# Second DFT step along S as products of 64x64 quadrants instead of 128x128 tables

## The chip, the cores and the metric

The kernel runs on one core of a Trainium2 chip. The metric is the time of one execution on the device in microseconds (us); the median of several runs is compared. The engines are named as in the profile: PE is TensorE (matmul), PEld its weight load, DVE is VectorE, ACT is ScalarE, POOL is GpSimd, and SP is SyncE, whose queue issues nearly all DMA transfers here.

## The reference, cut to what matters

One training step of a small network block, forward and backward, in bfloat16, with S = 2048 rows and D = 448 columns:

```
h   = x + irfft2(rfft2(layernorm(x)) * (w_r + 1j * w_i))        # part A, a spectral filter
h2  = h + B(layernorm(h))                                       # part B: MLP along S, 2048 -> 1792 -> 2048, gelu
outputs: h2, and the gradients of x, w_r, w_i, w1, b1, w2, b2 for a given grad_out
```

The transforms are two-dimensional: along D (448 points, real input, so 225 frequencies) and along S (2048 points). Part A needs one forward and one inverse transform in the forward pass, and one forward and one inverse transform again in the backward pass, where also the gradient of the filter is formed.

## The kernel before

**The DFT as matmuls.** The transform along S is split as 2048 = 128 x 16. A first step (`row_a`, `row_b`) does the part along D and one factor of the part along S, and its results go by DMA into the tile `D2`: 128 partitions, 16 groups, and per group a real and an imaginary row of 226 frequencies. The second step along S handles each of the 16 groups `g` by a table of its own: the real table `Vt[:, g, :]`, the imaginary table `Ut[:, g, :]` and the latter's negative `Un[g]`, each 128x128. A product with a complex operand is three matmuls that add into one PSUM buffer: 452 columns by V (real and imaginary part at once), then 226 columns by U and 226 columns by -U:

```
mm(pv, lhsT=Vt[:, g, :], rhs=D2[:, g, :, :], start=True, stop=False)
mm(pv[:, 0, :], lhsT=Ut[:, g, :], rhs=D2[:, g, 1, :], start=False, stop=False)
mm(pv[:, 1, :], lhsT=Un[g], rhs=D2[:, g, 0, :], start=False, stop=True)
```

In the order of rows and columns used here, the entries of a table that aren't zero are spread over the whole of it; most entries are zero. `gen_UV` builds Ut and Vt while the first step runs (16 masked copies of 128x256 elements at line 508 or 510, shared between DVE and ACT); `gen_inv_s` makes the inverse tables UTt, VTt from them by products with the permutation `permI`; `gen_neg` makes the negatives on DVE.

**The stage.** `s2_stage` runs this step twice, once in the forward pass (`make_inv` true) and once in the backward pass. It loops over `c2`, a pair of groups. In one turn it does the forward product of two groups, copies the result out of PSUM (`evac`) into `xs[c2]`, does the inverse product (`s2_inv`) of two groups that were multiplied by the filter some turns before, copies that out and sends it to `D3` by DMA. After this, `on_mult` multiplies a pair by the filter: `w_mult` is four `tensor_tensor` operations on DVE per pair, two of 904 and two of 452 elements per partition; in the backward pass there are four more for the filter's gradient. The multiplication of a pair follows `ml` turns after its forward product (`ML_F` = 4 in the forward pass, 0 in the backward pass), the inverse product two turns after that.

**What fills PE.** `fill(n)` takes the next n matmuls of a pending generator, here `dg_gen` (a product of part B's backward pass with w2, 224 matmuls of 448 columns) in the forward pass, and `gw_gen` (weight gradients, mostly 512 columns) in the backward pass. Each turn of the stage fills 2 x 3 matmuls in the forward pass, 2 x 8 in the backward pass. What is left of `dg_gen` runs after the stage (`drain`). Every engine's order is the order of the program's text, except POOL's, which a scheduler decides.

**Who copies.** `evac` puts each copy on ACT or DVE, whichever has the smaller estimated load so far; this is decided when the program is built. POOL isn't used by `evac`.

**The filter.** `w_load` brings w_r and w_i by eight DMA transfers into `W_rows`: four while the first step runs, and four at the start of the stage. `w_place` copies it into the order of the frequencies (`W_view_F`): 16 copies of 64 partitions x 900 elements, by `evac`, four per turn in turns 3 to 6. In the backward pass the filter comes back from memory (`w_d`), and the gradient is stored by eight transfers (`w_io`) from inside the last stage (`gx_consumer`, turns `GW_AT`).

Of the kernel before, what the change touches and what calls it, by code (L numbers as in the profile page):

```python
# [17 lines left out]
P = 128  # L18
# [6 lines left out]
NT = 16  # L25
# [97 lines left out]
def kernel(  # L123
# [98 lines left out]
    def v4(ap):  # L222
        return ap.rearrange("p (b c) -> p b c", b=4)
# [18 lines left out]
    Ut = mem.tile([P, NG, P], BF16, name="Ut")  # L242
    Vt = mem.tile([P, NG, P], BF16, name="Vt")
    UTt = mem.tile([P, NG, P], BF16, name="UTt")
    VTt = mem.tile([P, NG, P], BF16, name="VTt")
# [3 lines left out]
    permI = mem.tile([P, P], BF16, name="permI")  # L249
# [101 lines left out]
    for _ in range(26):  # L351
# [5 lines left out]
    gp_.iota(fr.rearrange("p (c q i g) -> p c q i g", c=2, q=2, i=4), pattern=[[1, 2], [8, 2], [16, 4], [2, 4]], base=0,  # L357
             channel_multiplier=0, allow_small_or_imprecise_dtypes=True)
# [72 lines left out]
    def gen_R(ve, sc):  # L431
        t = ftmp(2688, P).bitcast(I32)
        tv = t.rearrange("p (c h x) -> p c h x", c=4, h=2)
        f2 = fr.rearrange("p (c x) -> p c x", c=4)
        for h in range(2):
            ve.tensor_scalar(out=tv[:, :, h, :], in0=f2, scalar1=pcol, scalar2=96.0 + 32.0 * h, op0=ALU.mult, op1=ALU.add)
        ve.tensor_scalar(out=tv[:, 0, 1, 0:1], in0=pcol, scalar1=64.0, scalar2=96.0, op0=ALU.mult, op1=ALU.add)
        ve.tensor_scalar(out=t, in0=t, scalar1=127, scalar2=None, op0=ALU.bitwise_and)
        sc.activation(out=Rm[:], in_=t, func=ACT.Sin, scale=s128, bias=half_r)


    def decode(eng):
        a4, fc, s_, c_, f_ = col(), col(), col(), col(), col()
        floor_div(eng, a4, pcolb, 32)
        gp_madd(s_, a4, -32.0, pcolb)
        floor_div(eng, fc, s_, 4)
        gp_madd(s_, fc, -4.0, s_)
        gp_madd(s_, s_, 4.0, a4)
        floor_div(eng, c_, fc, 4)
        gp_madd(f_, c_, -4.0, fc)  # L450
        return fc, s_, c_, f_

    def masks(eng, c_, f_):
        msk, mk, k0, k1 = col(4), col(), col(), col()
        for j in range(4):
            eng.tensor_scalar(out=msk[:, j:j + 1], in0=f_, scalar1=float(j), scalar2=None, op0=ALU.is_equal)
        eng.tensor_tensor(out=mk, in0=msk[:, 0:1], in1=c_, op=ALU.mult)
        eng.tensor_scalar(out=k1, in0=mk, scalar1=-1.0, scalar2=1.0, op0=ALU.mult, op1=ALU.add)
        eng.tensor_tensor(out=k0, in0=mk, in1=msk[:, 0:1], op=ALU.subtract)
        eng.tensor_scalar(out=k0, in0=k0, scalar1=1.0, scalar2=None, op0=ALU.add)  # L460
        return msk, mk, k0, k1
# [3 lines left out]
    def gen_UV():  # L465
        _, s_, c_, f_ = rows = decode(gp_)
        nrow = col()
        gp_madd(nrow, rows[0], 16.0, s_)
        msk, mk, k0, k1 = masks(gp_, c_, f_)
# [12 lines left out]
        ve.tensor_scalar(out=permI[:], in0=krow[:, 0:P], scalar1=nrow, scalar2=None, op0=ALU.is_equal)  # L482
        ve.scalar_tensor_tensor(out=base[:, 0, :, 1], in0=fix, scalar=mk, in1=base[:, 0, :, 1], op0=ALU.mult, op1=ALU.add)
        for dst, o0, o1, pt in ((Ut, ou, ou, pu), (Vt, ov0, ov1, pv)):
            t = ftmp(1024 if dst is Ut else 2048, 16, 16, 2).bitcast(I32)
            for k, o in ((0, o0), (1, o1)):
                ve.tensor_scalar(out=t[:, :, :, k], in0=base[:, :, :, k], scalar1=s_, scalar2=o,
                                 op0=ALU.mult, op1=ALU.add)
                yield
            ve.tensor_scalar(out=t[:, 0, :, 1], in0=base[:, 0, :, 1], scalar1=s_, scalar2=pt, op0=ALU.mult, op1=ALU.add)  # L490
# [4 lines left out]
            sc.activation(out=comp, in_=t.rearrange("p g l c -> p (g l c)"), func=ACT.Sin, scale=s2048, bias=half_uv)  # L495
            yield True
            cv = comp.rearrange("p (g l c) -> p g l c", g=16, l=16)
            for c, k in ((1, k0), (0, k1)):
                ve.tensor_scalar(out=cv[:, 0, :, c], in0=cv[:, 0, :, c], scalar1=k, scalar2=None, op0=ALU.mult)
            yield  # L500
            d0 = dst[:, :, 0:64].rearrange("p g (l f) -> p g l f", f=4)
            d1 = dst[:, :, 64:112].rearrange("p g (l f) -> p g l f", f=3)
            for j in range(4):
                m = msk[:, j:j + 1]
                dj = d1[:, :, :, j - 1] if j else dst[:, :, 112:128]
                for o, c in ((d0[:, :, :, j], 0), (dj, 1)):
                    if load[1] + 0.24 < load[0] + 0.38:
                        ve.tensor_scalar(out=o, in0=cv[:, :, :, c], scalar1=m, scalar2=None, op0=ALU.mult)
                    else:
                        sc.activation(out=o, in_=cv[:, :, :, c], func=ACT.Copy, scale=m)  # L510
                    yield
# [7 lines left out]
    def gen_inv_s(h):  # L519
        src, dst = ((Ut, UTt), (Vt, VTt))[h // 4]  # L520
        g0 = 4 * (h % 4)
        pt = ps_ff()
        for i in range(4):
            mm(pt[:, i * P:(i + 1) * P], lhsT=src[:, g0 + i, :], rhs=permI[:], start=True, stop=True)
        evac(out=dst[:, g0:g0 + 4, :].rearrange("p g c -> p (g c)"), in_=pt[:])
# [37 lines left out]
    def w_io(Wv, dr, di, store):  # L563
        for c_, d in ((0, dr), (1, di)):
            for p0, p1, g0, g1, row, dims in ((0, 64, 0, 16, 0, [[16 * DF, 4], [1, 16 * DF]]),
                                              (64, 112, 0, 16, 112, [[-DF, 48], [1, DF]]),
                                              (112, 128, 1, 16, 127, [[-DF, 15], [1, DF]]),
                                              (112, 128, 0, 1, 64, [[1, DF]])):
                sb = Wv[p0:p1, g0:g1, c_, 0:DF]
                d_ap = bass.AP(d.tensor, d.offset + row * DF, [[P * DF, 16]] + dims)  # L570
                if store:
                    nc.sync.dma_start(out=d_ap, in_=sb)
                else:
                    nc.sync.dma_start(out=sb, in_=d_ap)
# [4 lines left out]
    def w_load():  # L579
        for c_, d in ((0, A_w_r), (1, A_w_i)):  # L580
            for p0, p1, j0, j1, row, dims in ((0, 64, 0, 16, 0, [[16 * DF, 4]]), (64, 112, 0, 16, 97, [[-16 * DF, 3]]),
                                              (112, 128, 0, 15, 113, []), (112, 128, 15, 16, 64, [])):
                nc.sync.dma_start(out=W_rows[p0:p1, c_, j0:j1, :],
# [4 lines left out]
    def w_place():  # L588
        for g in range(0, NG, 4):
            for c_ in range(2):  # L590
                for p0, p1, src in ((0, 64, W_rows[0:64, c_, g:g + 4, :]),
                                    (64, P, W_rows[64:P, c_, NG - 1 - g:(NG - 5 - g if g < 12 else None):-1, :])):
                    evac(out=W_view_F[p0:p1, g:g + 4, c_, 0:DF], in_=src)
                    yield
# [8 lines left out]
    Un = [r448[:, (NG + g) * P:(NG + g + 1) * P] for g in range(12)] + [rE[:, (3 * NT + g) * P:(3 * NT + g + 1) * P] for g in range(4)]  # L603
    UTn = cut(r448, 0, NG, P)
# [12 lines left out]
    blk_ring = ring(rS, 0, 2, 8, 2, 4, P // 4)  # L617
# [42 lines left out]
    def row_a(t, R):  # L660
# [7 lines left out]
        evac(out=blks[t // 4][:, :, :, t % 4, :], in_=pa[:].rearrange("p (a e b) -> p a e b", a=8, e=2))  # L668

    def row_b(h, quarters=False):  # L670
# [6 lines left out]
        for w in (1, 0):  # L677
            for b in range(2):
                if quarters:
# [769 lines left out]
```

## Time and profile before

| | us |
|---|---|
| median of 3 runs | 356.61 (356.28 to 357.08) |
| span of the profiled execution, first to last instruction | 355.2 |
| median of the runs less that span | 1.4 |
| PE busy in the span | 340.1 (96%) |
| DVE busy | 253.9 (71%) |
| ACT busy | 214.9 (61%) |
| POOL busy | 69.7 (20%) |
| second DFT step, forward pass | 49.5 to 80.5 of the span |
| second DFT step, backward pass | 252.9 to 298.3 of the span |

The profile is of one execution. No time of its own beyond the span is given for it, so the 1.4 us by which the runs' median exceeds the span stands for what lies around the span. The start of each instruction is recorded; a matmul's recorded duration contains its way through the array, so that the pace of a stream of matmuls is read from start to start: 452 columns take 0.191 us, 226 columns 0.096 us, 448 columns 0.188 us, 512 columns 0.216 us.

### The profile page before, as it was taken

The numbers are of one execution on the slowest core, as the hardware profiler recorded it, in microseconds if no ns is written. First come the engines' busy times: TensorE is split into PE (matmuls) and PEld (weight loads), VectorE is DVE, ScalarE is ACT, GpSimd is POOL, SyncE is SP. The second block draws the span as 40 slices with busy tenths as digits, with TensorE's granted clock in tenths as the row PEclk, the third lists the DMA queues.
The fourth block names the chain that finished last, engine by engine and source line by source line (L and its number), as shares of the span: only waits on it lengthen the run. The fifth ranks groups of instructions, "written<-read, shape, count | busy, mean of one in ns | idle before, by whom it ended". The sixth has DMA issues, their size and how long they took to land.

```text
span 355.2 us, 6479 instructions
## 1 busy us (share of the span) xinstructions
PE 340.1 (96%) x2147; PEld 184.2 (52%) x2147; DVE 253.9 (71%) x679; ACT 214.9 (61%) x458; POOL 69.7 (20%) x227
## 2 busy tenths in 40 slices
PE   7588999999999999999999999999999999999995
PEld 3355766555645555555555555544454544555642
DVE  8895638981884888776236988786595965499993
ACT  5469848964986545504322346666387766579872
POOL 6876000000220000001001111110000000067880
PEclk9999999999999999999999999999999999999999
DMA  8999979768999999997876999969966898799995
GB/s 196 284 190 244 212 186 184 139 170 279 285 288 352 297 350 230 246 235 213 209 171 149 184 219 190 206 158 304 295 177 193 231 233 248 230 198 284 209 303 221
DMA packets 147673, 81.64 MB, mean 230 GB/s; under 512 B 95480, under 2 KB 139768, under 8 KB 147384
## 3 DMA queue, kind: packets, MB, share of 16 engines
q1 hardware_dynamic: 147352, 80.83, 91.9%
q8 instruction: 17, 0.28, 0.3%
q10 hardware_dynamic: 288, 0.39, 0.3%
q14 instruction: 16, 0.13, 0.1%
HBM read 27.56 MB, written 23.89 MB: 145 GB/s over the span
## 4 chain that ended last, share of the span: by engine, by line
PE 82%; ACT 6%; POOL 5%; DVE 4%; issue 2%; DVEq 0%; ACTq 0%; POOLq 0%
PE ps_mm L218 68%; PE ps_ff L218 14%; ACT rO L82 2%; DVE r L82 1%; ACT rG L82 1%; ACT Ut L82 1%; DVE rA L82 1%; POOL cols L406 1%; POOL cols L407 0%; DVE rG L82 0%; ACT rX L82 0%; ACT rD L82 0%; ACT rAT L82 0%; ACT csI L82 0%; POOL nt_f L385 0%
## 5 line engine op out<-in xcount | busy, mean ns | idle before, releaser
L218 PEld LDWEIGHTS <-r 128*128 128x128 bf16 (+1 forms) x660 | 61.8, 104 | 50.0 <-issue 3.0
L218 PEld LDWEIGHTS <-rS 128*128 128x128 bf16 (+2 forms) x496 | 40.1, 97 | 37.8 <-issue 4.9
L218 PE MATMUL ps_mm<-rD,r 128*128 128x448 bf16 x224 | 44.5, 352 | 0.0
L82 ACT CAST rO<-ps_mm 128x512 bf16<-128x512 f32 (+1 forms) x66 | 35.2, 579 | 11.3 <-PE ps_mm L218 10.8
L218 PEld LDWEIGHTS <-rst 128*128 128x128 bf16 (+1 forms) x320 | 23.8, 97 | 29.0 <-issue 13.7
L218 PE MATMUL ps_mm<-rC,rE 128*128 128x448 bf16 x144 | 33.4, 352 | 3.2 <-DMA rC<-in_grad_out_dram 3.2
L218 PE MATMUL ps_mm<-r,rst 128*128 128x512 bf16 (+3 forms) x192 | 36.5, 353 | 0.0
L82 ACT CAST r<-ps_ff 128x452 bf16<-128x452 f32 x55 | 31.3, 577 | 7.3 <-PE ps_ff L218 6.2
L218 PE MATMUL ps_mm<-rB,r 128*128 128x448 bf16 x160 | 31.2, 352 | 0.1
L218 PE MATMUL ps_mm<-rG,rst 128*128 128x512 bf16 (+1 forms) x128 | 28.4, 380 | 0.0
L82 ACT ACTIVATE r<-ps_mm,rstd_h 128x448 bf16<-128x448 f32 x16 | 10.1, 634 | 26.8 <-PE ps_mm L218 26.8
L82 ACT ACTIVATE r<-rC 128x448 bf16<-128x448 bf16 x16 | 9.1, 570 | 26.7 <-DMA out_dram<-r 21.8
L82 DVE SCALAR_TENSOR_TENSOR r<-ps_mm,b2col,r 128x448 bf16<-128x448 f32 x16 | 10.9, 682 | 19.9 <-PE ps_mm L218 18.3
L82 ACT ACTIVATE rG<-rG 128x896 bf16<-128x896 bf16 x14 | 13.3, 950 | 14.9 <-DVE rG L82 14.7
L218 PE MATMUL ps_mm<-rE,rS 128*128 128x448 bf16 x112 | 21.5, 352 | 0.0
L218 PEld LDWEIGHTS <-rO 128*128 128x128 bf16 (+1 forms) x165 | 15.7, 98 | 10.9 <-ACT rO L82 0.2
L1179 POOL TENSOR_SCALAR lcol<-lcol 128x1 f32<-128x1 f32 x16 | 8.5, 532 | 64.7 <-ACT r L82 64.7
L82 ACT CAST rS<-ps_ff 128x512 bf16<-128x512 f32 x30 | 17.7, 592 | 4.3 <-PE ps_ff L218 4.3
L1370 POOL TENSOR_SCALAR lcol<-lcol 128x1 f32<-128x1 f32 x16 | 4.6, 287 | 76.5 <-ACT r L82 76.4
L218 PEld LDWEIGHTS <-rE 128*128 128x128 bf16 x148 | 14.0, 98 | 10.6 <-issue 3.7
L218 PE MATMUL ps_ff<-csI,rAT 113*128 113x224 bf16 (+1 forms) x108 | 19.0, 297 | 0.4 <-ACT rAT L82 0.2
L82 ACT CAST rG<-ps_mm 128x512 bf16<-128x512 f32 (+1 forms) x28 | 14.4, 550 | 8.1 <-PE ps_mm L218 8.0
(196 smaller groups left out, 667.0 us busy)
## 6 DMA issues: line engine op xcount, KB each, us to landing
out_dram<-rO SPq DMA_DIRECT2D x34, 256.0 KB
r<-in_B_w_dram SPq DMA_DIRECT2D x5, 1024.0 KB
r<-r SPq DMA_DIRECT2D x16, 226.0 KB
r<-r SPq DMA_DIRECT2D x32, 113.0 KB
rS<-in_B_w_dram SPq DMA_DIRECT2D x4, 896.0 KB
out_dram<-rG SPq DMA_DIRECT2D x10, 256.0 KB
rO<-in_B_w_dram SPq DMA_DIRECT2D x2, 1024.0 KB
w_d<-rG SPq DMA_DIRECT2D x1, 1808.0 KB
```

Of the source, the lines that this page charges most:

```text
L82: fn(**kw)
L218: nc.tensor.matmul(out, lhsT=lhsT, rhs=rhs, start=start, stop=stop)
L406: gp_.tensor_scalar(out=gtmp, in0=in0, scalar1=scalar, scalar2=None, op0=ALU.mult)
L1179: gp_.tensor_scalar(out=m1, in0=ms, scalar1=-1.0 / D, scalar2=None, op0=ALU.mult)
L1370: gp_.tensor_scalar(out=m1, in0=ms, scalar1=-2.0 / D, scalar2=None, op0=ALU.mult)
```

## The change

Rows and columns of the second step's tables are sorted so that each table is two 64x64 blocks instead of one 128x128 block, and all tables (`Ut`, `Vt`, `Un`, `UTt`, `VTt`, `UTn`) have 64 columns. Two groups `g` and `g + 4` are handled together (`duo_groups`): the 64 upper and 64 lower partitions of each are multiplied by their own 64x64 block, and the two groups are placed so that the four blocks lie in the four quadrants of PE's array: rows `r`, columns `r ^ a`, for `a` the group of the pair. A pair's product is 12 matmuls of a quarter of the array instead of 6 of the whole. The number of columns per matmul (452, 226, 226) is as before. `permI` has 64 columns too, and `gen_inv_s` uses quadrants.

`gen_UV` needs 2 masked copies of 512 elements per table instead of 8 of 256, all on DVE, and makes `Un` at once; the four `gen_neg` groups elsewhere are gone, and `UTn` is made once and kept. Its index arithmetic on POOL (`decode`, `masks`, the iotas of `fr` and `base`) has some operations more.

The frequencies stand in another order in the partitions. `w_load` has 12 transfers instead of 8, six of them at the start of the stage instead of four; the gradient's store (`w_store`) has 12 instead of 8. `w_place` has 32 copies of 32 partitions x 900 elements instead of 16 of 64 partitions x 900: 16 by `evac`, and 16, for the upper 32 partitions of each half, on POOL; four copies, those of one pair, are called in each of the turns 3 to 10. In a turn of `s2_stage` the forward product of the pair, then the inverse product, then twice `fill(n_fill)` follow, with `on_mult` between the two.

The core of the diff (index arithmetic, the order of the views in `row_a`, `row_b` and `bwd_mult`, and the transfers' address lists left out):

```
+    def quad(out, lhsT, rhs, start, stop):
+        nc.tensor.matmul(out, lhsT=lhsT, rhs=rhs, start=start, stop=stop)
+        clock[0] += int(np.prod(rhs.shape[1:])) / 9600.0
+    def half(i):
+        return slice(64 * i, 64 * i + 64)
+    def duo(v, n):
+        e, a, b = (2, 2, 4)
+        return v.rearrange("p (e a b) c k -> p e b a c k", e=e, a=a, b=b)[:, n // 4, n % 4]
+    def duo_groups(n):
+        g = 8 * (n // 4) + n % 4
+        return g, g + 4
...
-    Ut = mem.tile([P, NG, P], BF16, name="Ut")
...
+    Ut, Vt, Un, UTt, VTt, UTn = (mem.tile([P, NG, 64], BF16, name=n) for n in ("Ut", "Vt", "Un", "UTt", "VTt", "UTn"))
...
# gen_UV
-            for j in range(4):
-                m = msk[:, j:j + 1]
-                dj = d1[:, :, :, j - 1] if j else dst[:, :, 112:128]
-                for o, c in ((d0[:, :, :, j], 0), (dj, 1)):
-                    if load[1] + 0.24 < load[0] + 0.38:
-                        ve.tensor_scalar(out=o, in0=cv[:, :, :, c], scalar1=m, scalar2=None, op0=ALU.mult)
-                    else:
-                        sc.activation(out=o, in_=cv[:, :, :, c], func=ACT.Copy, scale=m)
-                    yield
+            for j, m in enumerate((m0, f_)):
+                ve.tensor_scalar(out=dst[:].rearrange("p g (m i) -> p (g m) i", i=2)[:, :, j], in0=comp, scalar1=m, scalar2=None,
+                                 op0=ALU.mult)
+                yield
+            if dst is Ut:
+                gen_neg(Un[:], Ut[:])
+                yield
...
     def w_place():
-        for g in range(0, NG, 4):
-            for c_ in range(2):
-                for p0, p1, src in ((0, 64, W_rows[0:64, c_, g:g + 4, :]),
-                                    (64, P, W_rows[64:P, c_, NG - 1 - g:(NG - 5 - g if g < 12 else None):-1, :])):
-                    evac(out=W_view_F[p0:p1, g:g + 4, c_, 0:DF], in_=src)
-                    yield
+        rows = W_rows.rearrange("p c (e a b) k -> p e b c a k", e=2, a=2)
+        dst = W_view_F.rearrange("p (e a b) c k -> p e b c a k", e=2, a=2)
+        for n in range(NG // 2):
+            e, b = n // 4, n % 4
+            for p0 in range(0, P, 32):
+                if p0 % 64:
+                    gp_.tensor_copy(out=dst[p0:p0 + 32, e, b, :, :, 0:DF], in_=rows[p0:p0 + 32, 1 - e, 3 - b, :, ::-1, :])
+                else:
+                    evac(out=dst[p0:p0 + 32, e, b, :, :, 0:DF], in_=rows[p0:p0 + 32, e, b])
+                yield
...
# s2_stage
+        def two(tables, n, rhs):
+            gs = duo_groups(n)
+            ps = [ps_ff()[:, 0:452].rearrange("p (c k) -> p c k", c=2) for _ in gs]
+            t0, t1, t2 = tables
+            for t, c, start, stop in ((t0, None, True, False), (t1, 0, False, False), (t2, 1, False, True)):
+                for a, g in enumerate(gs):
+                    for r in range(2):
+                        x, o = rhs(a, g, r), ps[a][half(r ^ a)]
+                        quad(o if c is None else o[:, c, :], lhsT=t[half(r), g, :], rhs=x if c is None else x[:, 1 - c, :],
+                             start=start, stop=stop)
+            run_due()
+            return ps
...
+            if c2 < nh:
+                pvs = two((Vt, Ut, Un), c2, lambda a, g, r: D2[half(r), g])
+                for a in range(2):
+                    evac(out=xs[c2][:, a], in_=pvs[a], scale=scale)
+            if c2 >= lag:
+                n = c2 - lag
+                y = ys.pop(n)
+                pvs = two((VTt, UTt, UTn), n, lambda a, g, r: y[half(r), a])
...
+            fill(n_fill)
+            if make_inv and c2 >= 3:
+                for _ in range(4):
                     next(wp, None)
...
             if ml <= c2 < nh + ml:
                 ys[c2 - ml] = on_mult(c2 - ml, xs[c2 - ml])
+            fill(n_fill)
...
-    for i in range(2):
-        gen_neg(UTn[:, 8 * i:8 * i + 8, :], UTt[:, 8 * i:8 * i + 8, :])
```

## The prediction

> **What bounds the kernel now.** The page comes first: busy time, the slices, the chain that ended last.
>
> ```profile
> PE 340.1 (96%) x2147; PEld 184.2 (52%) x2147; DVE 253.9 (71%) x679; ACT 214.9 (61%) x458; POOL 69.7 (20%) x227
> ...
> PE   7588999999999999999999999999999999999995
> ...
> DVE  8895638981884888776236988786595965499993
> ...
> PE 82%; ACT 6%; POOL 5%; DVE 4%; issue 2%; DVEq 0%; ACTq 0%; POOLq 0%
> ```
>
> PE is the bound nearly everywhere, so fewer matmul columns should shorten the kernel. But DVE is at nine tenths in slice 8, inside the second step of the forward pass. So I ask for busy time by stage (columns: window, length, then PE, PEld, DVE, ACT, POOL).
>
> ```profile
> 56.60:60.50 3.90, 3.90 (x28) 2.40 (x26) 3.78 (x9) 3.32 (x5) 0.00 (x0) 1.00 1.06 158
> 60.50:79.00 18.50, 17.61 (x110) 10.20 (x107) 16.97 (x38) 15.04 (x27) 0.71 (x2) 1.00 0.71 162
> ...
> 252.90:298.30 45.40, 45.40 (x261) 21.37 (x260) 33.66 (x70) 33.50 (x66) 0.00 (x0) 1.00 0.81 217
> ```
>
> The two uses of the step differ. In the backward pass PE is busy for all of 45.4 us and DVE for 74%: what PE saves there, the kernel saves. In the forward pass, from 60.5 to 79.0, DVE is busy for 92% and PE already waits. The groups of 49.5 to 80.5, and POOL's one long copy (from 162 us on), say what DVE does there:
>
> ```profile
> L82 DVE TENSOR_TENSOR rS<-rX,rG 128x904 bf16<-128x904 bf16 x16 | 9.3, 623 | 0.3
> L82 DVE TENSOR_TENSOR rS<-rS 128x452 bf16<-128x452 bf16 x16 | 5.6, 391 | 0.7
> L82 DVE COPY rG<-rB 64x900 bf16<-64x900 bf16 x9 | 3.5, 390 | 0.6 <-ACT rG L82 0.4
> ...
> L1157 POOL COPY rD<-rD 128x896 bf16<-128x896 bf16 x1 | 0.9, 937 | 10.4 <-DVE gb L82 10.4
> ```
>
> The eight filter multiplications take 14.9 us of DVE and end at 78.9 us; a copy of the filter takes 0.39 us there. The change gives POOL 16 such copies of 900 elements, and the trace shows a bar between POOL and DVE. The timeline at 318 us and at the start:
>
> ```profile
> 318.84 0.38 DVE L82 TENSOR_TENSOR r<-r,r 128x448 bf16<-128x448 bf16 x1
> 318.86 1.25 POOL L1385 TENSOR_SCALAR stats<-stats,lcol 128x1 f32<-128x1 f32 x1
> 319.14 0.61 DVE L82 CUSTOM_DVE_ANT_0 r<-r,rE 128x448 bf16<-128x448 bf16 x1
> 319.68 0.38 DVE L82 TENSOR_TENSOR r<-r,rA 128x448 bf16<-128x448 bf16 x1
> ...
> 320.56 0.34 POOL L1385 TENSOR_SCALAR stats<-stats,lcol 128x1 f32<-128x1 f32 x1
> ```
> ```profile
> 1.34 0.50 POOL L339 IOTA r<- 128x448 f32 x1
> 1.41 0.57 DVE L82 TENSOR_SCALAR r<-r,cols 128x64 int32<-128x64 f32 x2
> ...
> 2.34 1.11 DVE L82 TENSOR_SCALAR r<-r,cols 128x226 f32<-128x226 f32 x4
> ```
>
> The same POOL operation of one element takes 0.34 us at 320.56 and 1.25 us when three DVE operations with both inputs in SBUF stand over it; it ends as they end. The other way round, two DVE operations of 64 elements take 538 and 404 ns beside POOL's iota of 500 ns, while 226 elements take 319 to 356 ns at 2.34 us. They finish 0.11 and 0.14 us after the iota. So each shuts the other out, for most of its duration.
>
> **The change, part by part.** The profiled execution has a span of 355.2 us; the median of the runs is 1.4 us above it. The sum is made on the span, and the 1.4 us are added at the end.
>
> *Backward pass, matmuls.* One product of one group takes 0.191 + 0.096 + 0.096 = 0.383 us from start to start, a pair 0.766. Afterwards four quadrants run at once. No row shows quadrants; the nearest are the two-row-half matmuls of the weight gradients (64 rows, 512 columns), which start 3 to 4 ns apart in all 60 pairs, the next pair 223 ns later. So a pair's product takes 0.383 + 3 x 0.01 = 0.41 us: 0.355 less, for 8 forward and 8 inverse products 5.7 us. Ends: 0 if only two quadrants run at once, -5.7 if all four do. I take the end that the pairs of rows support.
>
> *Changes of the array's shape.* Each passage from full to half rows costs 98 to 100 ns beyond the columns' time, each return 94 to 96 ns, in all 30 cases of the trace. The stage has 10 turns backward, each with one stretch of quadrants between fills: 10 x 0.193 = +1.9 us. Backward pass together: -5.7 + 1.9 = -3.8. The multiplications' DVE work is unchanged, and 33.7 us of DVE and 33.5 of ACT fit into 41.6, so PE remains the bound.
>
> *Forward pass, matmuls.* The same -5.7, with 14 turns +2.7, is off the path: DVE and POOL set the end there, as follows. I count it at nothing; the cover is the queue of the next paragraph.
>
> *Forward pass, filter copies.* The last packets of w_i land at 56.6 us, and the first copy starts then; the six transfers of the change carry the same bytes, so POOL can't start earlier. (Two more issues of 0.6 us on SP delay it, the start of the stage may come a little earlier: nothing.) From there on DVE and POOL share what only one can use: DVE's multiplications 14.9 us; DVE's filter copies, of which the built order puts 11 of 16 on DVE, 11 x 0.39 = 4.3 us; POOL's copies, 16 x 0.94 us long. Each multiplication needs its pair's two POOL copies, so that neither can wait for the other's end. For the exclusive part of a copy I take 0.8 us: the iota let DVE finish 0.11 us after its end, and such a small DVE operation itself takes about 0.2 us, so its hold ended some 0.1 us early. Sum: 12.8 + 14.9 + 4.3 = 32.0 us, and the last multiplication ends at 56.6 + 32.0 = 88.6 instead of 78.9: +9.7. What PE does after that shrinks: before, two products of 0.383, 16 fills of 0.188 us between and behind them to 82.8 (3.8 us); after, one pair and the same fills, 0.41 + 3.0: -0.4, near enough -0.5 with the copies' ends. Forward pass: +9.2. Ends: with no exclusion DVE needs only 19.2 us from 56.6 + 0.8 (its wait for the first multiplication's inputs), thus 76.6, and the stage gains 2.3 + 0.5 = 2.8; with the whole 0.94 us held it is 16 x 0.14 = 2.2 more, +11.4.
>
> The Trainium skill states the rule for this in "SBUF — State Buffer", section "SBUF: two separate sides": the port pair that DVE and GpSimd share is locked by one of them for a whole instruction. By that page the copies would hold 0.94 us each and the kernel would take 364.2; the trace shows it for short POOL operations and for one iota, not for a copy.
>
> *First step.* ACT loses 11 copies of 0.85 us for Ut and Vt; DVE's become 4 of about 0.6 us instead of 5 of 0.42. That removes PE's wait of 1.48 us at 29.45 us (ACT's copies stood ahead of the eviction). POOL's longer index arithmetic, some 8 operations of 0.2 us more, delays the first rstd that DVE waits for: up to 1 us back. Neither reaches the end, since the stage's queue starts with the filter's landing at 56.6: 0, ends -1.5 and +1.0.
>
> *The rest.* The removed negatives (0.84 us of DVE at 190 us, 0.84 at 250) lie beside a fully busy PE: nothing. Four more stores cost SP four issues of about 0.6 us, spread over 12 turns of the last stage: nothing, at most +0.6 where an output of x stands behind one. The tables' inverse products take 32 matmuls of 128 columns at 57 ns now, 1.8 us; as 32 pairs of quadrants bounded by 25 to 57 ns, with changes of shape, the same within 0.5.
>
> Sum: 355.2 + 9.2 - 3.8 = 360.6 us of span, 362.0 with what lies around it.
>
> **The rivals.** *POOL's copies cost nothing* (faster). For it: the trace has no long POOL copy beside a DVE multiplication, and the one at 162 us ran at 0.94 us over DVE work that reads PSUM. Against it: the 1.25 us row and the iota. Then -2.8 - 3.8 = -6.6: 350.0. The point that decides is what a copy holds: the forward pass changes by 16 h - 3.6 us, which meets the 3.8 gained backward at h = 0.46 us.
>
> *Quadrants don't run four at a time* (slower still). For it: only row halves are seen, never two column halves, and each pair of them writes two different PSUM buffers, while the change lets both row halves write one. If they run by twos, nothing is gained backward and the passages stay: 355.2 + 1.4 + 9.2 + 1.9 = 367.7. One at a time, the 16 pairs take 0.766 more each than before, 379.9.
>
> The skill speaks against the change here: "TensorEngine Tiling (Array Packing)", section "Restrictions and Gotchas", says that different row tiles can't access the same PSUM bank at the same time. By it the two quadrants of one group would follow each other, which is the case of twos; by the rows alone it is the case of four. I keep to the rows, since the two halves of a buffer lie in different partitions, and no run here shows this.
>
> **How the numbers follow.** My forecast, copies that shut DVE out with four quadrants at once, has 0.58; copies that cost little 0.25; quadrants by twos or singly 0.13; the rest, among it copies with odd strides that take longer, 0.04. Forecast: 362.0. By its bounds alone it lies between 358 (hold of 0.6 us, -3.2, and half of the first step's gain) and 366 (hold of 0.94 us, stores, a smaller gain backward). The range reaches to the rival's 350 and to the twos' 368: 350 to 368. 0.2% is about what a measurement here can tell from no change. Faster: the 0.25 and a little of the forecast's low edge, 0.26; within 0.2%: 0.02; slower: 0.72.
>
> **What would show it.** In the changed profile POOL's 16 copies should lie between 56 and 88 us, many longer than 0.94 us, and the first multiplications of a pair should lengthen from 0.62 towards 1.4 us; the last one ends near 88.6, and PE shows idle time of some 12 us there, put down to DVE. In the backward stage 41.6 us instead of 45.4, four quadrants within some 12 ns, 10 passages. I am wrong if the multiplications end before 79 us with copies beside them, or if quadrants start 0.1 us or more apart.

## The result, and the profile after

The changed kernel takes 367.75 us (median of 4 runs, 367.26 to 368.09) where the kernel before takes 356.44 us (4 runs beside it, 356.00 to 357.08): 1.0318 times as long, with a 95% interval of 1.0301 to 1.0334, so 11.3 us more. The profiled execution took 367.26 us with a span of 365.5, which is 10.3 more than the span before.

The page of the changed kernel, the same lines as before:

```profile
PE 336.0 (92%) x2363; PEld 173.0 (47%) x2371; DVE 257.4 (70%) x671; ACT 205.9 (56%) x444; POOL 85.1 (23%) x251
...
PE   7679996484999999999999999999999999999996
...
DVE  7887436399279388877622688787497984399993
...
PEclk9999999769999999999999999999999999999999
...
PE 21%; issue 0%; DVEq 0%; DVE 0%
```

PE's busy time fell by 4.1 us, and its share from 96% to 92%: PE now waits. The slices show where. The seventh to tenth slice of PE (55 to 91 us; one slice is 9.1 us) read 6, 4, 8, 4; before, all four were 9. The granted clock drops in two of them. The chain can be followed only over a fifth of the span here, so the stages must be read one by one. Busy time of the changed kernel by stretch (window, length, then PE, PEld, DVE, ACT, POOL, clock, DMA share, GB/s):

```profile
56.60:63.30 6.70, 4.26 (x50) 1.79 (x48) 3.94 (x6) 2.56 (x5) 6.42 (x8) 1.00 1.08 209
63.30:69.60 6.30, 3.67 (x30) 1.32 (x30) 2.23 (x5) 3.31 (x7) 1.14 (x3) 0.73 0.55 122
69.60:79.90 10.30, 5.27 (x34) 1.98 (x35) 7.79 (x14) 2.76 (x7) 4.12 (x5) 0.67 0.30 73
79.90:93.10 13.20, 7.91 (x80) 3.19 (x77) 12.21 (x21) 7.13 (x14) 4.09 (x4) 1.00 0.27 73
...
262.00:306.30 44.30, 43.51 (x356) 17.02 (x364) 33.71 (x71) 34.53 (x69) 0.00 (x0) 1.00 0.87 228
```

In the forward pass no engine is busy throughout. From 63.3 to 69.6 DVE works for 2.2 of 6.3 us and POOL for 1.1: that is waiting, not a full port. Backward PE is nearly as full as before (43.5 of 44.3 us). This last window isn't cut at the same matmuls as the one of 45.4 us in the prediction, so that the two lengths don't tell what the stage saves; the table at the end of this section does.

The groups of the stretch from 49 to 94 us:

```profile
L82 DVE TENSOR_TENSOR rS<-rX,rG 128x904 bf16<-128x904 bf16 x16 | 9.4, 626 | 9.4 <-POOL rG L608 8.8
L82 DVE TENSOR_TENSOR rS<-rS 128x452 bf16<-128x452 bf16 x16 | 8.6, 576 | 0.7
L82 DVE COPY rG<-rB 32x900 bf16<-32x900 bf16 x11 | 7.5, 683 | 0.2
```
```profile
L608 POOL COPY rG<-rB 32x900 bf16<-32x900 bf16 x16 | 15.6, 988 | 21.3 <-DVE rS L82 10.6 <-DMA rB<-in_A_w_i_dram 10.3
```

Two things stand in these lines. DVE's multiplications of 452 elements went from 391 to 576 ns and its copies from 390 to 683 ns: the same work per partition, longer beside POOL. The multiplications of 904 elements, which the prediction expected to lengthen, did not (623 and 626 ns): here POOL's copies ran while DVE stood, or beside what DVE does after them. And two idle times name a partner: DVE stood 8.8 us for POOL's copies, and POOL's copies stood 10.6 us for DVE. Each engine waited for the other. POOL's own timeline, and the two waits of DVE (start, duration, then the idle time ahead in brackets):

```profile
56.12 1.83 POOL L608 COPY rG<-rB 32x900 bf16<-32x900 bf16 x2 [10.25 <-DMA rB<-in_A_w_i_dram]
...
58.31 4.93 POOL L608 COPY rG<-rB 32x900 bf16<-32x900 bf16 x5
66.39 0.20 POOL L844 CAST b1col<-smc 128x16 f32<-128x16 bf16 x1 [3.15 <-DMA smc<-rst]
68.59 0.20 POOL L844 CAST b2col<-smc 128x16 f32<-128x16 bf16 x1 [2.01 <-DMA smc<-rst]
68.86 2.82 POOL L608 COPY rG<-rB 32x900 bf16<-32x900 bf16 x3
73.01 2.15 POOL L608 COPY rG<-rB 32x900 bf16<-32x900 bf16 x2 [1.33 <-DVE rS L82]
82.36 1.98 POOL L608 COPY rG<-rB 32x900 bf16<-32x900 bf16 x2 [7.20 <-DVE rS L82]
86.44 2.22 POOL L608 COPY rG<-rB 32x900 bf16<-32x900 bf16 x2 [2.10 <-DVE rS L82]
```
```profile
63.27 1.17 DVE L82 TENSOR_TENSOR rS<-rX,rG 128x904 bf16<-128x904 bf16 x2 [2.73 <-POOL rG L608]
...
71.71 1.17 DVE L82 TENSOR_TENSOR rS<-rX,rG 128x904 bf16<-128x904 bf16 x2 [6.11 <-POOL rG L608]
```

Between the seventh and the eighth filter copy POOL's queue holds two casts that have nothing to do with the filter: `turn_biases` turns the biases b1 and b2 by two transposing DMAs and casts the result on POOL, and it is called in turn 4 of the stage. The casts wait for those DMAs, which SP issues only after 63.94 us. So POOL stood from 63.24 to 68.86, except for 0.4 us of casts, and the second multiplication stood 6.11 us for copies behind the casts. The kernel before has the same two casts, with nothing behind them that anybody waits for in this stage:

```profile
68.38 0.43 POOL L823 CAST b1col<-smc 128x16 f32<-128x16 bf16 x1 [16.01 <-DMA smc<-rst]
69.20 0.28 POOL L823 CAST b2col<-smc 128x16 f32<-128x16 bf16 x1 [0.38 <-DMA smc<-rst]
```

The order of POOL's copies explains why the second multiplication needed them. In the built program they stand as pairs 0, 4, 0, 4, 1, 5, 1, then the casts, then 5, 2, 2, 3, 3, 6, 6, 7, 7. A pair is two groups, g and g + 4, and the waits in the program go by the address range from the first to the last element: the range of pair 1 (groups 1 to 5) contains pair 2's first group, so the multiplication of pair 1 waits for the copies of pair 2 as well, and the copies of pair 2 wait for the multiplication of pair 0 (groups 0 to 4) to have read. The order and the ranges are read from the program; the waits in the traces fit them, and an experiment below takes the ranges apart.

The quadrants themselves do what was forecast. The timeline of PE in one turn of the backward pass:

```profile
282.62 0.39 PE L223 MATMUL ps_ff<-r,Vt 64*64 64x452 bf16 x4
282.83 0.27 PE L223 MATMUL ps_ff<-r,Ut 64*64 64x226 bf16 x4
282.93 0.27 PE L223 MATMUL ps_ff<-r,Un 64*64 64x226 bf16 x4
283.03 0.36 PE L223 MATMUL ps_ff<-rS,VTt 64*64 64x452 bf16 x4
```

A pair's product takes 0.41 us from the first to the next product's start, four quadrants starting within 8 to 13 ns of the first in all 48 groups of four of the stage.

Where the time went, from the same matmul of the same stream in both traces:

| | before, us | after, us | later by |
|---|---|---|---|
| first product of the second step, forward | 49.74 | 48.97 | -0.77 |
| last multiplication ends | 78.9 | 93.0 | +14.1 |
| last matmul of `dg_gen` that fills PE | 85.64 | 99.47 | +13.83 |
| last matmul that reads rD and r, ahead of the backward stage | 234.68 | 248.51 | +13.83 |
| last matmul on r and rS, behind the backward stage | 339.47 | 349.81 | +10.34 |

So the forward pass lost 13.8 us including what the first step gained, everything between the stages is equal to 0.01 us, and the backward pass gained 3.5.

### The profile page after: what moved, and what is told of

Its sections match the earlier page's. It is cut to its first block, busy times and chain, and to the rows that moved or that the text cites. A ratio compares the mean times of both kernels' runs of the same rounds, so it can differ in the third digit from the quotient of the medians.

```text
span 365.5 us, 6963 instructions
## 1 busy us (share of the span) xinstructions
PE 336.0 (92%) x2363; PEld 173.0 (47%) x2371; DVE 257.4 (70%) x671; ACT 205.9 (56%) x444; POOL 85.1 (23%) x251
## 5 line engine op out<-in xcount | busy, mean ns | idle before, releaser
L218 PEld LDWEIGHTS <-r 128*128 128x128 bf16 (+2 forms) x600 | 55.8, 105 | 44.9 <-issue 2.9
L82 ACT CAST rO<-ps_mm 128x512 bf16<-128x512 f32 (+1 forms) x69 | 36.9, 583 | 12.8 <-PE ps_mm L218 10.0
L82 ACT CAST r<-ps_ff 128x452 bf16<-128x452 f32 x56 | 30.3, 576 | 18.1 <-PE ps_ff L223 13.1
L218 PE MATMUL ps_mm<-rG,rst 128*128 128x512 bf16 (+1 forms) x123 | 27.3, 380 | 0.6 <-issue 0.3
L223 PE MATMUL ps_ff<-rS,VTt 64*64 64x452 bf16 x64 | 6.4, 392 | 15.4 <-DVE rS L82 15.2
L608 POOL COPY rG<-rB 32x900 bf16<-32x900 bf16 x16 | 15.6, 988 | 21.3 <-DVE rS L82 10.6
L218 PE MATMUL ps_mm<-rC,rO 128*128 128x448 bf16 x80 | 19.8, 378 | 0.0
```

Source lines behind the costliest of these rows:

```text
L82: fn(**kw)
L218: nc.tensor.matmul(out, lhsT=lhsT, rhs=rhs, start=start, stop=stop)
L223: nc.tensor.matmul(out, lhsT=lhsT, rhs=rhs, start=start, stop=stop)
L608: gp_.tensor_copy(out=dst[p0:p0 + 32, e, b, :, :, 0:DF], in_=rows[p0:p0 + 32, 1 - e, 3 - b, :, ::-1, :])
```

## The experiments

**Taking the biases out of POOL's way.** One line moved:

```
-        if c2 == 4:
-            turn_biases()
...
     s2_stage(fwd_x, fwd_mult, ML_F, 3, 24, True)
+    turn_biases()
     drain()
```

> The changed kernel with the turning of the biases (two transposing DMAs and the two casts that POOL makes of their result) called after the second step instead of in its turn 4. In the profile of the change POOL's queue stands for 5.6 us (63.24 to 68.86) at these casts, ahead of its 8th filter copy, and the second multiplication waits 6.11 us for a copy behind it. Theory A (waits inside POOL's queue made the forward pass 4.6 us worse than forecast): the second multiplication starts near 66.5 instead of 71.7 us, everything after it moves up by as much, 362.5 us. Theory B (DVE and POOL simply share one port for longer than the forecast's 32 us, and the casts only fill time that POOL would have lost anyway): the last multiplication still ends near 93, 367 to 368 us.

Measured: 363.66 us (363.44 to 363.84), ratio to the kernel before 1.0208 (1.0193 to 1.0224); 4.1 us less than the change. POOL's timeline of this kernel:

```profile
58.49 5.75 POOL L608 COPY rG<-rB 32x900 bf16<-32x900 bf16 x6
65.39 2.14 POOL L608 COPY rG<-rB 32x900 bf16<-32x900 bf16 x2 [1.15 <-DVE rS L82]
69.22 2.15 POOL L608 COPY rG<-rB 32x900 bf16<-32x900 bf16 x2 [1.69 <-DVE rS L82]
78.57 1.98 POOL L608 COPY rG<-rB 32x900 bf16<-32x900 bf16 x2 [7.19 <-DVE rS L82]
```

The second multiplication starts at 67.92 instead of 71.71, and the last one ends at 89.2 instead of 93.0. Theory A holds, theory B falls: 4.1 of its 4.6 us are back. The long wait of 7.19 us, which copies of pair 6 have for an earlier multiplication, is still there and costs nothing to be seen: DVE shows no idle time ahead of the multiplications that need these copies.

**Taking the address ranges apart.** The filter by pairs in SBUF, and read back by groups for the backward pass:

```
-        dst = W_view_F.rearrange("p (e a b) c k -> p e b c a k", e=2, a=2)
+        dst = W_view_F.rearrange("p (e b a) c k -> p e b c a k", e=2, a=2)
...
-        return w_mult(c2, xc, W_view_F, False)
+        return w_mult(c2, xc, W_view_F[:, 2 * c2:2 * c2 + 2], False)
```

> The changed kernel with the filter laid out by pairs in SBUF: the two groups of a pair, g and g + 4, stand next to each other, so that the address range of one pair holds no group of another; the load of the filter for the backward pass reads it back by groups. In the change POOL's copies of the pairs 2, 3, 6 and 7 wait for a multiplication of an earlier pair, and multiplications wait for copies of the next pair. Theory A: these waits go, POOL makes 15 copies in one go from 56.1 to about 71 us, the biases' casts stand only before the 16th; the first multiplication starts near 65.5 (after the ninth copy), the last ends near 88 if a copy shuts DVE out for 0.8 to 1.0 us each, 362 us; near 84.5 and 359 us if copies cost DVE nothing. Theory B (port alone, longer than forecast): still near 93 and 367.

Measured: 363.55 us (363.45 to 363.66), 4.2 us less than the change; the last multiplication ends at 88.9. The casts stand behind 15 copies now and run at 71.7 us without a wait. The two transposing DMAs of the biases are still at their place in SP's queue here, so that it was POOL's queue, not SP's, that cost the change its 4 us. The time is some 1.5 us above the 362 expected. The backward pass, with its filter read back by groups, has 0.5 us of that: the stream between the table's last two marks is 101.77 us long here and 101.30 in the change.

**Both together.**

> Both edits together: filter by pairs in SBUF, biases turned after the second step. Theory A: as with the filter by pairs alone, within 1 us (the casts stood before the last copy only, and that one is needed last): 361 to 362 us. If the two waits were independent costs that add up, it would be 5 us less than either alone. Theory B: 367.

Measured: 363.40 us (363.33 to 363.55), ratio 1.0202 (1.0187 to 1.0217). The gains of the two edits don't add up: 4.1, 4.2, and together 4.35. It was one wait that needed both parts: a copy that stands behind the casts, and an early multiplication that wants it. Taking away either is enough. In this kernel POOL never stops:

```profile
56.11 7.65 POOL L608 COPY rG<-rB 32x900 bf16<-32x900 bf16 x8 [10.15 <-DMA rB<-in_A_w_i_dram]
...
64.08 8.79 POOL L608 COPY rG<-rB 32x900 bf16<-32x900 bf16 x8
```
```profile
65.04 2.61 DVE L82 TENSOR_TENSOR rS<-rX,rG 128x904 bf16<-128x904 bf16 x2 [4.74 <-POOL rG L608]
67.69 2.05 DVE L82 TENSOR_TENSOR rS<-rS 128x452 bf16<-128x452 bf16 x2
```

The last multiplication ends at 88.9, and `dg_gen` is 9.7 us later than before. This is close to what the prediction had summed up (88.6 and +9.2), but by another road, and the closeness is luck: the scheduler puts the eight copies of the partitions 96 to 127 first, so that DVE stands 4.74 us for the ninth copy, and after that seven copies run beside its multiplications and double them (two of 904 elements in 2.61 us instead of 1.17). No run has POOL's copies in the order of the pairs, so that how much of this is the order alone stays open.

**What a copy on POOL costs DVE by itself.** The kernel before with one added POOL copy behind each of its 16 filter copies, into a part of SBUF that nobody reads:

```
                     evac(out=W_view_F[p0:p1, g:g + 4, c_, 0:DF], in_=src)
+                    gp_.tensor_copy(out=spare[p0:p0 + 32], in_=src[0:32])
```

> The kernel before the change, with one POOL copy of 32 partitions x 900 elements added behind each of its 16 filter copies, into a part of SBUF that nobody reads and for which nobody waits. It measures by itself what such copies cost DVE. The forecast's term is 16 x 0.8 us = 12.8 us in a stretch where DVE is busy for 92%: the last multiplication would end near 90 instead of 79 and the kernel take 367 to 369 us. If a copy and a multiplication run beside each other freely: 356.4 us, no difference. A value between tells the hold of one copy: (time less 356.4, plus some 1.5 us of DVE's idle time there) / 16.

Measured: 364.42 us (364.38 to 364.67), 8.1 us more than the kernel before, 356.29 in these rounds (ratio 1.0232, 1.0216 to 1.0247). The scheduler put eight of the copies in one go behind the biases' casts, and five of the 16 outside the stretch of DVE's multiplications and copies. POOL and DVE there:

```profile
69.51 8.91 POOL L595 COPY r<-rB 32x900 bf16<-32x900 bf16 x8
```
```profile
69.61 2.12 DVE L82 TENSOR_TENSOR rS<-rS 128x452 bf16<-128x452 bf16 x2
71.76 2.52 DVE L82 TENSOR_TENSOR rS<-rX,rG 128x904 bf16<-128x904 bf16 x2
74.38 1.98 DVE L82 TENSOR_TENSOR rS<-rS 128x452 bf16<-128x452 bf16 x2
76.39 2.51 DVE L82 TENSOR_TENSOR rS<-rX,rG 128x904 bf16<-128x904 bf16 x2
```

DVE needs 9.13 us for work that takes 2 x 0.70 + 2 x 1.17 = 3.74 us alone: 5.4 us for eight copies, 0.67 each. The last multiplication ends at 85.9 instead of 78.9: 6.9 us over the 11 copies inside the stretch, 0.63 each (0.66, if the 0.33 us are added by which the second step starts earlier in this trace). Nobody waits for these copies, so this is what they cost by running beside DVE, with no wait in it. "Copies cost DVE nothing" is excluded. "A copy holds DVE for all its duration" is too: it lasts 0.92 us alone and 1.11 us here.

**The change without POOL's copies.** The rows that POOL reversed are loaded from memory straight into their place, in pieces of 450 bytes:

```
-                    (96, 128, 1, 0, 16, 81, [[-16 * DF, 2]]), (33, 64, 2, 0, 16, 97, []),
-                    (32, 63, 2, 0, 15, 113, []), (32, 63, 2, 15, 16, 64, [])):
+                    (96, 128, 1, 0, 16, 96, [[-DF, 32]]), (33, 64, 2, 0, 16, 112, [[-DF, 16]]),
+                    (32, 63, 2, 1, 16, 127, [[-DF, 15]]), (32, 63, 2, 0, 1, 64, [])):
+                if p0 % 64:
+                    nc.sync.dma_start(out=W_view_F[p0:p1:ps, j0:j1, c_, 0:DF],
...
                 if p0 % 64:
-                    gp_.tensor_copy(out=dst[p0:p0 + 32, e, b, :, :, 0:DF], in_=rows[p0:p0 + 32, 1 - e, 3 - b, :, ::-1, :])
+                    pass
```

> The changed kernel without POOL's filter copies: the filter rows of the partitions 32 to 63 and 96 to 127 are loaded from memory straight into their place and order (pieces of 450 bytes instead of up to 7200), and only the 16 copies by ACT and DVE stay. Same result, same quadrants. If POOL's copies are the whole cost of the forward pass (by the port and by the waits), it must come out as the prediction's first rival: DVE needs only its 19.2 us, the last multiplication ends near 77 to 79 us, about 350 to 353 us, faster than the kernel before. If the quadrants or the new layout cost something of their own there, it stays above 356. A risk beside: the transfers in small pieces may land later than 56 us, while all 16 DMA engines are busy.

Measured: 355.98 us (354.31 to 357.70), ratio 0.9986 (0.9965 to 1.0006): no difference from the kernel before that can be told, and 12 us less than the change. The seventh multiplication waits 2.64 us for a filter copy on ACT, for which the next experiment offers an explanation:

```profile
74.21 1.20 ACT L82 CAST r<-ps_ff 128x452 bf16<-128x452 f32 x2 [2.84 <-PE ps_ff L223]
...
75.72 0.94 ACT L82 COPY rG<-rB 32x900 bf16<-32x900 bf16 x1
```
```profile
76.70 1.17 DVE L82 TENSOR_TENSOR rS<-rX,rG 128x904 bf16<-128x904 bf16 x2 [2.64 <-ACT rG L82]
```

Without that wait it would be near 353.3, just above the 350 to 353 expected. The same with the biases turned late:

> The same, and the biases turned after the second step. POOL has no filter copies in its queue here, so that nothing should wait behind the casts: the same time as without it, within 0.5 us. In the change the same edit alone was worth 4.1 us.

Measured: 352.35 us (352.20 to 352.79), ratio 0.9885 (0.9870 to 0.9900). It beats both kernels, the one before by 4.1 us. The expectation "no difference" was wrong by 3.6 us, for POOL's queue was not the only one that the biases stand in. SP's queue without and with the later biases:

```profile
65.82 2.48 SPq L847 DMA_TRANSPOSE smc<-rst  x2
68.40 1.95 SPq L306 DMA_TRANSPOSE rO<-in_B_w_dram  x1
70.46 7.83 SPq L750 DMA_DIRECT2D r<-r  x10
```
```profile
65.63 1.98 SPq L306 DMA_TRANSPOSE rO<-in_B_w_dram  x1
67.71 10.30 SPq L750 DMA_DIRECT2D r<-r  x13
```

The two transposes take 2.48 us of SP, and the transfers of the inverse products to `D3` (L750) start 2.75 us later behind them. The copies out of PSUM go through a ring of eight buffers that these transfers empty. By 70.3 us eight such copies are done in both kernels; the ninth starts at 74.21 in the first and at 71.84 in the second, with ACT's filter copy behind it. That the ring is what held ACT is read from this order and isn't shown by an experiment of its own: the profile puts the 2.84 us down to PE, whose product for this copy had started at 71.19 and ended before 71.8.

**POOL's copies put back, for nobody.** The same kernel as the first of these two, with 16 POOL copies into a part of SBUF that nobody reads:

```
-                    pass
+                    gp_.tensor_copy(out=spare[p0:p0 + 32].rearrange("p (c a) k -> p c a k", c=2), in_=rows[p0 - 32:p0, e, b])
```

> As the kernel that loads these filter rows straight into place, with POOL's 16 copies of 32 x 900 elements put back, but into a part of SBUF that nobody reads: no multiplication waits for them, and none of them waits for one. In the kernel before, 11 such copies moved the last multiplication by 6.9 us, 0.63 us each. Here it should be as many times 0.63 us as copies lie beside DVE's work, at most 10 us, over the kernel without them. The rest of what the change lost is then waits, not the port.

Measured: 360.02 us (359.73 to 360.34), 4.0 us over the kernel without them. The last multiplication ends at 85.0 instead of 80.7; the wait of 2.64 us has gone into it, since DVE is late itself. Against the kernel with late biases, which has no such wait (78.2), it is 6.8 us. Twelve of the copies lie inside the stretch, 0.57 us each: a copy beside DVE costs about as much in the changed kernel as it did in the kernel before.

**The copies on ACT and DVE.**

```
-                    gp_.tensor_copy(out=dst[p0:p0 + 32, e, b, :, :, 0:DF], in_=rows[p0:p0 + 32, 1 - e, 3 - b, :, ::-1, :])
+                    evac(out=dst[p0:p0 + 32, e, b, :, :, 0:DF], in_=rows[p0:p0 + 32, 1 - e, 3 - b, :, ::-1, :])
```

> The changed kernel with POOL's 16 copies given to ACT and DVE like the other 16. No copy on POOL is left, so no port is shared, but there are 32 copies of 32 partitions where the kernel before had 16 of 64. DVE takes about half of the added ones at 0.39 us (+3 us), ACT the rest at 0.85 us. Port and queue waits as the cause: the last multiplication ends near 82 to 84, 355 to 359 us. If the number of copies were the cause, whoever makes them: near 363.

Measured: 356.93 us (356.51 to 357.65), ratio 1.0014 (1.0005 to 1.0024); the last multiplication ends at 82.7. As expected (355 to 359 us, 82 to 84). The same 32 copies with none on POOL take 10.8 us less than the change, and 6.5 less than the version with nothing in POOL's way (363.40). The number of copies is not the cause; the engine is.

**All filter rows straight into place.** The rows of the partitions 0 to 31 and 64 to 95 too, and no copy left:

> The changed kernel with all filter rows loaded from memory straight into place (no filter copy on any engine), and the biases turned after the second step. With half of them loaded so it took 352.4 us, and PE still waited 3.8 us for DVE, whose copies of the filter are 4.3 us of the stretch. If DVE's queue is still what sets the end of the forward pass: 3 to 4 us less, 348.5 to 350 us. If the transfers in pieces of 450 bytes land too late, or PE becomes the bound at once, 351 to 353.

Measured: 352.79 us (351.74 to 353.72), no better than half of them (352.35). The multiplications do end 2.9 us earlier, at 75.3, but PE now waits for transposes of w2 (1.8 us) and for the biases (1.5 us): the transfers set the end, and the gain of DVE is lost to them. That DVE's queue still set the end was wrong; the other expectation was right.

**The biases late in the kernel before.** The control for the first edit:

> The kernel before, with the biases turned after the second step only. A control: the casts stand alone in POOL's queue there, and DVE, not SP, sets the pace: 356.4 us, within 0.7. If it were faster by some 4 us, the edit would be worth the same without the change, and the 4.1 us seen in the changed kernel would not be POOL's queue.

Measured: 356.63 us (356.12 to 357.18), ratio 1.0008 (0.9995 to 1.0021): the same. The 4 us were the change's own.

**Full tables with all rows straight into place.** The kernel before with `w_io` as the filter's load, no filter copies, biases late:

> The kernel before, full 128x128 tables, with all filter rows loaded straight into place and the biases turned after the second step: the counterpart of the changed kernel so edited, so that the two differ by the quadrants, the smaller tables and the order of frequencies alone. DVE loses its filter copies (4.3 us) and ACT its five, and PE becomes the bound of the forward pass: 353 to 355 us. The quadrants' own worth is then the difference to the other one: by the sums of the prediction -5.7 + 1.9 backward and -5.7 + 2.7 forward, 5 to 7 us where PE is the bound in both passes, 3.5 to 4 where it is so in the backward pass only.

Measured: 360.78 us (359.56 to 361.40), ratio 1.0121 (1.0084 to 1.0158): slower, and outside of what was expected. PE waits 3.0 us for a transpose of w2, and the fourth multiplication starts 4.84 us after the third instead of 2.0. It loads all rows in small pieces while the DMA engines are full, so it doesn't separate the quadrants from the transfers. The changed kernel with all rows straight into place (352.79) takes 8.0 us less; 3.5 of these are the backward pass, and the rest, forward pass and transfers, isn't taken apart. No run has full tables with half of the rows loaded so, and what the quadrants are worth in the forward pass stays open. In the backward pass the picture is nearly the same in all versions with quadrants: between the two marks of the table around it the stream takes 104.79 us before and 101.3 in the change and in the versions without filter by pairs, 3.5 us less; with the filter by pairs it is 3.0 and 3.2 less.

## Why the prediction was right and wrong

The direction was right, the reason in part, the size was not: 362.0 us was forecast (5.4 over the kernel before), 367.75 came (11.3), inside the range of 350 to 368. By its steps:

- *Backward pass.* Forecast -5.7 + 1.9 = -3.8, measured -3.5. The pair's product takes the forecast 0.41 us. The passages cost 93 ns in (309 ns to the first quadrant where 512 columns take 216) and 93 ns out (189 instead of 96, from the last quadrant), wherever the matmul before them is of full height and the next one is recorded; taken in the same way, the half-row passages of the kernel before are 96 and 92, where the prediction has 98 to 100 and 94 to 96; ten times each that is 1.86 against 1.9 us. The products' 16 x 0.355 us less these make 3.8; where the other 0.3 us went isn't known.
- *Quadrants by twos.* Excluded. The sentence of the Trainium skill, "TensorEngine Tiling (Array Packing)", "Restrictions and Gotchas", that different row tiles can't access the same PSUM bank at the same time doesn't hold for halves of one buffer in different partitions: here both row halves write one buffer within 13 ns of each other, to different 64 partitions, and the 12 matmuls of a pair take 0.41 us. That the measured 367.75 us meets this rival's 367.7 is chance.
- *The port.* That POOL's copies hold up DVE was right: they lengthen its operations in every run that has them. The size was 0.8 us a copy in the sum; beside DVE's work it is 0.57 to 0.67 us. By the skill's rule ("SBUF — State Buffer", "SBUF: two separate sides", the pair locked for a whole instruction) it would be 0.92 to 0.98 us, an estimate from the time that a copy takes, which the runs don't show. The rival that copies cost nothing is excluded.
- *The forward filter copies: the step that failed.* It was forecast as +9.2 us, with the last multiplication at 88.6. Measured +13.8 and 93.0. Two terms were wrong, in opposite ways. The hold was summed as 12.8 us, but DVE's multiplications and filter copies took 25.5 us in the change (the three groups above) and 19.2 in the version without POOL's copies (352.35), so the copies lengthened DVE's work by 6.3 us. The wait was put at nothing, and DVE stood 8.8 us for copies. The other 2.2 us of the 36.5 us from 56.5 to 93.0 are two of DVE's copies out of PSUM and short idle times, which the sum left out. With either the casts or the interleaved ranges out of the way it is +9.7 to +10.0 and 88.9 to 89.2; that this meets the forecast is luck, for with both gone it is made of 6.4 us of longer work and 4.7 us of standing. Left out were the biases' casts, which the trace of before shows on POOL at 68.38 us, waiting for a DMA, and into whose queue the change moves 16 copies that multiplications wait for. Together with the ranges of interleaved pairs this is 4.35 of the 5.75 us by which the forecast fell short. The sentence that failed is "Each multiplication needs its pair's two POOL copies, so that neither can wait for the other's end": multiplications waited 8.8 us for copies, and copies 10.6 us for multiplications.
- *The rest of the shortfall.* The span came out at 365.5 instead of 360.6: 4.6 us of that is the forward pass and 0.3 the backward pass. The median is 2.2 us above the span where 1.4 was taken from the kernel before. In each run on record the time is 1.7 to 1.9 us above the span of the same execution. The 1.4 came from a median and the span of another execution: by these 1.7 to 1.9 us, the profiled span of 355.2 belongs to the slowest of the three (357.08). The profiled execution of the change is the fastest of its four; the others have spans up to 0.8 us longer, at a lower mean clock (0.975 to 0.977 against 0.986).
- *First step.* Zero was taken, with ends of -1.5 and +1.0; the second step starts 0.8 us earlier than in the profile before (48.97 against 49.74). Not all of this is the change's: in the three other profiles with the old first step it starts at 49.06 to 49.41. As forecast it hardly reaches further, for POOL's copies start with the filter's landing (56.1 us, where 56.6 was taken).
- *Forward matmuls as worth nothing.* Consistent with the traces, since DVE released PE's waits in all versions with copies on POOL; not separated by an experiment.

Put together from the runs: without POOL's copies the quadrants and the direct load make the kernel 4.1 us faster (352.35), nearly all of it in the backward pass (3.5 us; the last matmul of `dg_gen` starts at 84.62 us, and at 84.95 in the kernel before with late biases); with POOL's copies and nothing in their way it takes 11.05 us more (363.40; the two differ in the load and in the filter's layout too), and the wait behind the biases adds 4.35 us (367.75).

## What to carry to other kernels

Before work is moved to a queue that "has time", list what stands in that queue in the stretch and what each of these waits for: an instruction of 0.2 us that waits for a DMA delayed 9 copies and through them the kernel by 4 us. An engine that shares a port with the bound of a stage isn't free for it, even at 23% busy: 16 copies on POOL cost the kernel more than the same 16 spread over ACT and the bound itself. Interleaved slices of one tile make waits between pieces that share no element; a layout in which what belongs together stands together takes them away.

## What was not expected of the hardware

Around a long wait of PE its granted clock falls to half and stays there for a while after it. The changed kernel by 2 us, the columns as above:

```profile
62.00:64.00 2.00, 0.00 (x0) 0.00 (x0) 0.72 (x2) 0.00 (x0) 1.18 (x2) 1.00 0.88 199
...
66.00:68.00 2.00, 2.00 (x10) 0.59 (x12) 0.00 (x0) 1.13 (x3) 0.20 (x1) 0.50 0.05 10
...
74.00:76.00 2.00, 1.59 (x14) 0.66 (x15) 1.88 (x4) 0.59 (x2) 1.11 (x2) 0.50 0.00 0
76.00:78.00 2.00, 1.78 (x9) 0.51 (x11) 1.90 (x5) 0.92 (x2) 0.00 (x0) 0.50 0.19 48
```

PE waited 4.4 us until 65.2 and 5.5 us until 74.4. After the first the granted clock fell at 65.95, during the second at 72.77, and it was 0.50 until 69.4 and 79.6: six fills of 448 columns took 2.26 us from 65.74, and at full clock 1.31. In the faster version (352.35), whose longest wait of PE in the stage is 0.9 us, it stayed at 1.00. The Trainium skill ("TensorE: Matmul & The Clock Gate", "Part 1: The HAM clock gate") states this as half the clock after an idle window of about 3.4 us; the two waits of 4.4 and 5.5 us agree. But in the kernel before with spare copies the clock was 0.50 from 77.0 to 80.5 us though PE's longest wait there was 2.6 us, and PE was busy for 0.9 of the 3.4 us ahead of the fall, so no idle time of 3.4 us in one piece was needed there. The prediction had left the clock out. Here DVE was the bound behind the waits, and what the low clock cost is not measured.
